# Another stored order for the same 1505 operations: 115 transfers and 451 engine operations move, 24 PSUM evictions change engine

## The chip, the cores and the metric

One core of one Trainium2 chip runs the whole kernel. The metric is the device time of one execution in microseconds (us). Times of before are three runs; one further execution was profiled.

## What is computed

Two independent layers on 2048 tokens of 640 channels, written side by side into one output of 2048 x 1280 (bfloat16).

- Layer A is a convolution layer. `k` goes through a causal filter of four taps per channel, is multiplied by `v`, then convolved along the sequence with a filter of full length (`ssm_k`, one per channel; the reference does it by FFT), a skip term `ssm_D` is added, and the result is multiplied by `q`.
- Layer B is segmented attention with a memory: 32 heads of 20 channels, four segments of 512 tokens. In each segment causal softmax attention within the segment is mixed, by a gate per head, with a read of a memory matrix that sums `phi(k) v` over the earlier segments (`phi(t)` is `t + 1` for positive t, else `exp(t)`).

```python
kv = k_shift * v                                   # A: short filter, then gate
y = irfft2(rfft2(kv_pad) * rfft2(ssm_k_pad))[:S] + kv * ssm_D
a = q * y
p = softmax(qs @ ks.T * scale + mask); a_dot = p @ vs     # B, one segment, one head
num, den = phi(qs) @ M, phi(qs) @ z + 1e-6
o = g * num / den + (1 - g) * a_dot
M += phi(ks).T @ vs; z += phi(ks).sum()
b = concat_heads(o) @ wo
```

## The kernel before

**Work.** Layer A is done in five blocks of 128 channels (`conv(dp)`, dp 0 to 4). A block loads `k` transposed into the tile `kr`, `v` into `vt`, the long filter into `kT`, runs the short filter as matmuls on TensorE (`ks`), transforms both signals with matmuls against the table `Wf` (`FX` for the signal, `FK` for the filter; eight PSUM results of 128x512 each, copied into the one buffer `F`), joins them with butterfly adds (`BX`, `BK`) and multiplies them (`P1` to `P3`, `YB`) on VectorE, and transforms back with `Wi` (`I`), times `q`. Layer B is done in eight units u (segment u // 2, head half u % 2). `project(u)` makes keys and queries (`P`, into `KQ`), values (`V`, into `Va`), transposes `KQ` by DMA into `KQT` (`KT`, one transfer for each of four token blocks t), makes the `phi` tiles and transposes them (`PT`), finds a bound for each key row, writes that bound into four strips of `KQT` by four small transfers (`rows`, one for each group of four heads), and updates the memory. `attend(u)` fills logits in PSUM by matmuls of 32 rows (`S`; three kinds: D for the diagonal, A and J for what lies below it), takes their exp on ScalarE into one of seven `ET` buffers, and multiplies with the values (`O`), then normalises on VectorE (`N`). `project_out(s)` transposes the segment's output (`oT`, by DMA; `ot` on TensorE in the last segment) and multiplies it with `wo` (`W`); `OB` stores it.

**Order.** The program does not call the engines while it walks these loops. A recorder notes all 1505 operations and what each one needs (`Recorder.add`, line 155). Then `Recorder.issue` (line 252) emits them in the order of a stored list (`ORDER`, line 996, compressed text). Every instruction of the page therefore stands at line 261. Each engine, and the one queue SP that issues nearly all transfers (201; four more go by POOL), runs its own instructions strictly in that order and waits at the head of its queue until what the instruction needs is there. A second list (`BASE`, line 1017) says which of the eight PSUM banks each of 471 groups of PSUM results uses: a group's first matmul waits until the group that had the bank before has been read. A third text (`EVICT`, line 993) has a digit for each of 227 copies from PSUM to SBUF (`evict`, line 405): 1 puts it on VectorE, 0 on ScalarE.

**Names.** An operation is named by its key and unit: `P/0/1` is the projection of unit 0, token block 1; `FK` and `FX` results are named by c from 0 to 3; `xt/0` to `xt/3` are the transposes of the first 512 rows of x on TensorE, whose copies make `xT`; `taps` is the four-tap filter transposed, from which ScalarE makes the filter matrices `skd`. Ten matmuls on zeros (`warm`) run at the start.

Of the kernel before, what the change touches and what calls it, by code (L numbers as in the profile page):

```python
# [995 lines left out]
ORDER = r"""
c-jrtgMttW5Czb=Gk0=rwrjI(+um&3wry{=YqM?Jwr#$5zT#w+Y?57aNKVNmxh0R}l_(NXTtrGs6^SI}q@v`L>Jn9=NgOF7p(MXlmGV+nk_aWQR+7{bAQdE|RFeV{Sqe%KEhI&?uv8XEKCPs6rKXsuRMxIiTWU#W
Ni5MNro@oa8cWJ(eyt%v(p?H@LP;gXw2qY3G*Vw`YC~x*^`x9;k=D{uifcCs(gxB<+DZ!vEw!|<l$177TboKh=^^bTtyIx;Qc-(J9c?9bwU0EBdfH6VOM5A$9i^(ql_FAH3Tl6;p*^Lr_LjcVLCWhO=_CWBn8cG|
l3cpT2<a@brG(Vi1d>RGNJA|u4K%C_mN7C=hRY~PDPd%s43)7mTB>OyEupJ*yo{6yQb>b!gErRcx<}S%d?~3-wTaHry|PjlX$tA4$t076lL|UfR%vscB$H)|?2`~(tW#yPY?AI;N@mDL-7l?lnrzbPazK`751p$s
rL`{AHabt6X<PlJEwsHJm6qB;=W9EiC0pg7bkd&MOBZNIJtlp1wj7qux=jwrHr=jAq__6bwc16y>Kxgj+hv^|my6O*Pe`!r)M2_=FUeI|p$m1m_SY>sK(EPMiDM&lr^K~gx>YaBX_+VEb-rAYcy>mX%Pxs(6Lp|2  # L1000
kli{#<J%57FN1WCuGif%Mx$A38>fq8uP&6NwnZ+;GTo<R^{gzG!MaSA>p3~5`!%Jdv7tIdPs&n>k5rb-qT6vjpp$f(PS;a1QV(i)nXEDFzKqsUn%Ex7bD5$`WQNYv>oQeu$qKn4H|4e**2j{>?#L{CDR<?NX0{`m
!B)#reIT<n0UpU~c_nM)jjWVJc2QqQR768Uq_DTLN)jQXWwQ11L@wz&$zoUZvOblha!sE}R@)$JB{9-lcDt&lb)CGIVV1)_N-`uzY&)w@bhw?-50V5S@>DlUPCKE`^ppl7DRS8-IjK`@gq_o=Hqr)KbX?FBh#<H1
yymvg5(9ZHrp2<<_#$bM#|GIqiHSS<Q19wjNrUV9NMqr#-q4$x4!884=CeMCjkkJVze|35pg&~1^|v^9r|<QZCbzU!!0yQ}iHiZ26|XhWe##roh<JFeza^bzLT3Dx43f>p+8>!<FSMY&)C86dAM}g<laKmU$5=uO
g-@CVpS7fY(}_0DfYO#8-!(J@KeUu(fFV03SxV$U8B2wqTGkZPtgscbB38+!8&S?8ps4jjWgBJ1tcp1zA}2;$aVuf7E!YNIE_A{Wt7>5|%Vt;}6h}3yZecOgCR+*Au-qt$APa|@79Qm-5{hAt<;7g9VEIrUg;5rz
QPE0bp1ri%))xVoZ-G+BDxe(dS`jR?0jOuStPB=eJ1d3yRuBQ~U_&iG8rV8pZ0)VJ^+!WnZ(t!Tu`rCxwicUhOxeOJVyO*8SjJ%#4na$+gk`qeMxd2d!3vAYMm7kQF%-iv5-V+i4Mt;YYE8`eTZf}6R#`QWG1=V4
U>us+Sj6H6tAUL+9^n`n9j%jvXJ-qs1YB)vY^`;%C@@RNuJ%{E8LczA+g9sg|Fox7M=$Gb+pLd?ZMXRB&P42Mn=A<va|$+FKXZ#j*cR)CP!@xCFqFG3G?TI)doTinFpSB$$EKn`yJG_O+78=i1+d?0;(-0piHOKR
*2Y1L#va&ZJFN@i@{mPmEhOU^i^qHDz&^Z-!`2gZ(3L58&d%B;>&trR#*`d|RJ>xBZ5q<B7mnHt)W<P9V#n=-rDjLY#7V1*(Ku!2tv9Bl0WMlZYY68gq-AKkV4>I*H!K~S;-=lQ!3?nG7{c2Y+3uKHW8AgLxM%Hn
)goDYUbFjXg!IhJ>z0uN*pv5dEHiOAnxGj@+hWYZ1AAnT?THQIQ=5%B2xFr-kip2pUR;9VoQs9%#0;E=wFqmYxdJ1&2wC~edb2Yh+Ip<R7`8)pF2xf(w`^R7hse!w+<<3zfc6;Ayd24ie2Ud*fjnG^HCTm7e2yG!
gPhF8`MANB$j1c;L4HnV7q-F_w#6k}Mr%x^djW>>f}GAG6feZ0gim8(7Go6Kh#7og#aW4=eI{REGfJ>BH=zpuvLv^lBevotI-mx__&5Gz5P$GHtFk74avQ4gJxg-}w__H|uq?~*Bdhb3T|q6DVtIbx96rJhd}19|
U@))ZG3K&1>vA?Dcmp<MBhF(*?!+}T<~O`S6E<aie!(vMVLgVk>-dhhXvRg{jfNi4!`oMUwi{^97Hr8@T+Hykg!8!vk-Rl;;<bITM*h*%7jgk3`&Yh#`7N~JC+x#gwq<*#f3nwjhbSK8x3Qe-xEB#@89R7XU(cGp  # L1010
9~&6L6?~7+*vMn}fK{yJoA?o{xsnI4mSH`bH}i0Q5NmiGwLQAOvwdvt@9hWnv%VkTQT)Ua1b7VJ%q`r?ZQRZV9@7uwAY=I<9O7ZN^&Q;FuNK=|czoZ@Jv@QE{DseK=dN-5H;(Wx{@@D(^dwsPQ6A$dgwns3*#F_p
{}GDkyLcM^40?)@HHp8qq#oDLK((uzez4O#i{tF#)Dt|zvka>z+0D-}wAS-5dY(NziiX#4n!qD!R6U2D9zoCJ7ZZ6Tji$-`0u%ZV>*W{O*?%*-CikBf=$CkzSD3<6`EN_<S9y(ptc~aQ>x`+ry^mi+L2v3Yw6Ul5
0^ZNRSsG90!t|cOGkR=|rD^@UHSs*2*ZX=t&*c5Rm1p(=UdV5<h+n`XX7y~I-Q#Kw&*FtWr^nG>*4m5uV?N+*=JMiR!i)Js-r^v?!%{xPOM4kF>*YM2j`Nb9+XwmtkFR%G-k-375BBl?ibMS#6KW;D&(}<#!@aUs
@$O#HhxrJv>Q7n66KN8y<|BQSKjUamtj}53$9Q$`=t;GcPxRC})?aXnPxVRulGA*;FZap*hRJk>ukac^(--<m-|ve(xz6@rpW}1=Ef4q-Po=Ybk*CzXo>7;28lC6!eV?!O6q-|)`38T-OuF7fe4{V$O&+MZbd_)R
b-u+9`XNuN>2$T{(af4&*Z5Z7=2>;S@9=E8(|7r9&!C5Wk00@io<(!(ZNKD4J-Z(B9D2s@_+7u}_x-G&^YebeFZ&h0>eu|b-|(A$%a8jBKk29ZwEqW|<?eI
"""
# [76 lines left out]
```

## Time and profile before

| what | value |
|---|---|
| three runs | 268.25, 268.42, 270.69 us; median 268.42 us |
| span of the profiled execution (first to last instruction) | 266.3 us |
| what lies around the span, if that execution took the median | 2.1 us |
| busy: TensorE matmul, VectorE, ScalarE, GpSimd | 257.8, 247.1, 248.8, 7.6 us |
| granted TensorE clock | 1.000 |

The page gives one time of its own, the span; the difference to a run's time lies before the first and after the last instruction. The busy times are unions: where one instruction starts before the last has left the engine, the overlap counts once. The chain is the list of work followed back from the last instruction, each step to what released it. A row of the timeline has the start, the time that the merged instructions took, the engine, the line, the operation, the tiles, and how many there are; an idle time before it and what ended it stand in brackets. The queue SP is SPq.

### The profile page before, as it was taken

Reading aid. Unit: us, or ns where it says so; the run is one execution under the profiler, and the core shown is the slowest. Engines: PE = TensorE matmul, PEld = TensorE weight load, DVE = VectorE, ACT = ScalarE, POOL = GpSimd, SP = SyncE. Lnnn points to the kernel's source line nnn. Section 1 sums busy time; section 2 is a strip of 40 time slices with the busy share of each in tenths; the row PEclk is TensorE's granted clock in tenths of the full one; section 3 lists DMA queues with packets and bytes.
Section 4 is the critical chain, followed back from the end, with each engine's and each line's share of the span. In section 5 each row is a group of like instructions: output and inputs, shape, how many; then the busy total and the mean of one; then the engine's idle time right before and its main releaser. Section 6 shows DMA issues by size and latency. Waiting matters only on the chain.

```text
span 266.3 us, 10034 instructions
## 1 busy us (share of the span) xinstructions
PE 257.8 (97%) x4323; PEld 193.0 (72%) x4323; DVE 247.1 (93%) x387; ACT 248.8 (93%) x392; POOL 7.6 (3%) x20
## 2 busy tenths in 40 slices
PE   7999999999999999999999999999999999988994
PEld 3788678778777778877767777778776876665871
DVE  0599999999999999999999999999999999999971
ACT  2878999999999999999999999999999999999953
POOL 8300000000000000000000000000000000000000
PEclk9999999999999999999999999999999999999999
...
GB/s 217 292 214 218 197 180 187 126 233 205 172 200 175 142 180 162 173 154 126 154 173 201 164 185 182 211 107 113 181 186 3 29 158 149 87 108 128 28 66 116
DMA packets 126604, 41.84 MB, mean 157 GB/s; under 512 B 114107, under 2 KB 125376, under 8 KB 126432
## 3 DMA queue, kind: packets, MB, share of 16 engines
...
## 4 chain that ended last, share of the span: by engine, by line
PE 62%; ACT 28%; DVE 5%; issue 2%; DMA 1%; POOL 0%; DVEq 0%; ACTq 0%; POOLq 0%
PE ps L261 62%; ACT ET L261 19%; ACT F L261 3%; ACT KQ L261 1%; ACT PP L261 1%; DMA qabs<-in_A_shift_k_dram 1%; ACT Va L261 1%; DVE vt L261 1%; ACT outb L261 1%; DVE Y L261 1%; DVE Kh L261 1%; ACT qabs L261 1%; DVE pq L261 0%; ACT xT L261 0%; DVE o L261 0%
## 5 line engine op out<-in xcount | busy, mean ns | idle before, releaser
L261 ACT ACTIVATE ET<-ps 128x1024 bf16<-128x1024 f32 x160 | 162.6, 1122 | 0.4 <-PE ps L261 0.2
L261 PEld LDWEIGHTS <-xT 128*128 128x128 bf16 x640 | 57.3, 98 | 27.8 <-issue 6.8
L261 PE MATMUL ps<-wqkv,xT 128*128 128x320 bf16 x480 | 77.0, 299 | 0.4
L261 ACT CAST F<-ps 128x512 bf16<-128x512 f32 x72 | 43.3, 686 | 0.9 <-DVE F L261 0.8
L261 PE MATMUL ps<-Va,ET 128*128 128x21 bf16 x1280 | 41.8, 173 | 0.0
L261 PEld LDWEIGHTS <-ET 128*128 128x128 bf16 x1280 | 39.1, 96 | 2.1 <-issue 1.0
L261 PE MATMUL ps<-KQT 32*128 32x128 bf16 (+3 forms) x896 | 35.7, 239 | 0.3
L261 PEld LDWEIGHTS <-Wf 128*128 128x128 bf16 x320 | 29.8, 98 | 6.1 <-issue 1.3
L261 ACT CAST KQ<-ps 128x320 bf16<-128x320 f32 x54 | 25.5, 513 | 2.4 <-PE ps L261 2.3
L261 PE MATMUL ps<-wo,xT 128*128 128x320 bf16 (+2 forms) x160 | 25.5, 299 | 1.3 <-ACT ET L261 1.3
L261 PEld LDWEIGHTS <-KQT 32*128 32x128 bf16 (+1 forms) x896 | 16.1, 92 | 9.9 <-issue 8.2
L261 PE MATMUL ps<-kT,Wf 128*128 128x256 bf16 x160 | 21.8, 273 | 0.1
L261 PE MATMUL ps<-vt,Wf 128*128 128x256 bf16 x160 | 21.2, 273 | 0.0
L261 PE MATMUL ps<-Y,Wi 128*128 128x256 bf16 x160 | 20.8, 273 | 0.0
L261 DVE TENSOR_TENSOR o<-ps,rr 128x640 bf16<-128x640 f32 x24 | 19.7, 819 | 0.4
L261 DVE TENSOR_TENSOR Y<-Y,pq 128x2048 bf16<-128x2048 bf16 (+1 forms) x20 | 18.6, 937 | 0.0
L261 PE MATMUL ps<-Mbd,PqT 128*128 128x84 bf16 x96 | 18.3, 203 | 0.1
L261 DVE TENSOR_TENSOR pq<-Xh,Kh 128x2048 bf16<-128x2048 bf16 x15 | 18.2, 1215 | 0.0
L261 PE MATMUL ps<-skd,kr 128*128 128x128 bf16 (+4 forms) x124 | 17.9, 270 | 0.0
L261 PEld LDWEIGHTS <-kr 128*128 128x128 bf16 x124 | 15.6, 147 | 2.5 <-issue 0.8
L261 PEld LDWEIGHTS <-Wi 128*128 128x128 bf16 x160 | 14.8, 98 | 2.5 <-issue 0.6
L261 ACT ACTIVATE PP<-KQ 128x1280 bf16<-128x1280 bf16 x12 | 15.9, 1361 | 0.0
...
## 6 DMA issues: line engine op xcount, KB each, us to landing
...
```

The lines of the kernel that those rows point to most:

```text
L261: f(*[fix(a) for a in args], **{k: fix(v) for k, v in kw.items()})
```

## The change

Nothing is computed otherwise and no instruction is added or removed, except that a copy on the other engine is another instruction there. Three stored texts are replaced:

```diff
-EVICT = ("10100001110000001000000010000000000000000000000000000000000000100000000000001000010001001010100110100000000000000000110000000000000010000000"
-         "000000000101000100100100000000000000010000001100001000000000000000000000010110010000100")
+EVICT = ("01001011001001000000010000000000000000000000000000000000000000100000000000001000010001001100110010100010000000000000010000000000000011000000"
+         "000000000101000100100100000000000000010000001000101000000000000000000000010110000000001")
 ORDER = r"""
-c-jrtgMttW5Czb=Gk0=rwrjI(+um&3wry{=YqM?Jwr#$5zT#w+Y?57aNKVNmxh0R}l_(NXTtrGs6^SI}q@v`L>Jn9=NgOF7p(MXlmGV+nk_aWQR+7{bAQdE|RFeV{Sqe%KEhI&?uv8XEKCPs6rKXsuRMxIiTWU#W
...
+c-jTQ17HvU6a>(_kF;zr+qP}DY}>YN+t#veEZes2_o5&xA|N6np)?$k0aQUYltV?NLTY434&+2G<VGIkMH*y8K2%43ltEM!Ks1y^RTM%s6hU4oh){@$@`!~>$b@{77?s3OSt_822#QK&lolc>YNIIXA`yzC4vLAQ
...
 BASE = r"""
...
```

Decoded and set beside the old lists:

- **EVICT.** 12 copies go from ScalarE to VectorE: xt/0, xt/3 (640 wide); kt/1, two of `FK`, one of `FX`, W/3/4 (512); P/0/0, P/0/1, P/1/0, P/2/3, W/2/2 (320). 12 go from VectorE to ScalarE: taps (40); xt/1 (640); kt/3, two of `FK`, one of `FX`, ot/3/2, W/3/2 (512); P/0/0 and P/0/2 (the other half of each), W/0/0, W/2/1 (320).
- **First 30 us.** On SP the first block of x goes from third place to first, so that the weights of `P` and then `ident` follow it; the four loads of `Wf` go 3, 1, 0, 2 in place of 3, 0, 2, 1. On TensorE xt/0 and the last of `warm` go ahead of `taps`, the gate's small matmul comes right behind `taps`, P/0/0 stays in its place with xt/1 and xt/2 behind it, and the second result of P/0/0 goes from ahead of `FK` to behind the short filter. ScalarE begins with the copy of `taps`, then the two exps of the gate, three `skd`, the copies of xt/1 and xt/2; before it began with one `skd`, xt/0, another `skd`, xt/3, the gate. On VectorE the four `ks` products come before the second of the `BK` steps.
- **Middle.** The order of the logits blocks `S` on TensorE is kept; between them the other matmuls are exchanged over a few places. 387 of 471 groups have another bank. On SP 95 of the 201 transfers are out of their old order, by up to 18 places: the transfer KT/3/0 goes from behind the copies and loads of block 3 (place 88) to between the first and the second `rows` of unit 2 (place 70), and of these four the one for head group 0, which was first, is now third, behind it; KT/4/0 goes behind four more copies of the filter of block 3 and the store OB/0/1; PT/3/3 goes from ahead of `rows` of unit 3 to behind them; oT/0/2 goes behind PT/4/3. On ScalarE one copy of P/5/0 into `KQ`, which needs KT/4/0 to have read that tile, goes five places ahead.
- **End.** The parts of the last `W` run in the order 2, 4, 3, 0, 1 (before 2, 4, 1, 3, 0), their stores likewise; I/2 goes ahead of ot/3/2 and I/0.

More of the change, by code (lines that the diff above doesn't have):

```diff
@@ L995 @@
 KQW, FW, WW = 1, 1, 1
 ORDER = r"""
-c-jrtgMttW5Czb=Gk0=rwrjI(+um&3wry{=YqM?Jwr#$5zT#w+Y?57aNKVNmxh0R}l_(NXTtrGs6^SI}q@v`L>Jn9=NgOF7p(MXlmGV+nk_aWQR+7{bAQdE|RFeV{Sqe%KEhI&?uv8XEKCPs6rKXsuRMxIiTWU#W
-Ni5MNro@oa8cWJ(eyt%v(p?H@LP;gXw2qY3G*Vw`YC~x*^`x9;k=D{uifcCs(gxB<+DZ!vEw!|<l$177TboKh=^^bTtyIx;Qc-(J9c?9bwU0EBdfH6VOM5A$9i^(ql_FAH3Tl6;p*^Lr_LjcVLCWhO=_CWBn8cG|
-l3cpT2<a@brG(Vi1d>RGNJA|u4K%C_mN7C=hRY~PDPd%s43)7mTB>OyEupJ*yo{6yQb>b!gErRcx<}S%d?~3-wTaHry|PjlX$tA4$t076lL|UfR%vscB$H)|?2`~(tW#yPY?AI;N@mDL-7l?lnrzbPazK`751p$s
@@ L1000 @@
[L1000 to L1012, printed above, removed]
@@ L1013 @@
-0^ZNRSsG90!t|cOGkR=|rD^@UHSs*2*ZX=t&*c5Rm1p(=UdV5<h+n`XX7y~I-Q#Kw&*FtWr^nG>*4m5uV?N+*=JMiR!i)Js-r^v?!%{xPOM4kF>*YM2j`Nb9+XwmtkFR%G-k-375BBl?ibMS#6KW;D&(}<#!@aUs
-@$O#HhxrJv>Q7n66KN8y<|BQSKjUamtj}53$9Q$`=t;GcPxRC})?aXnPxVRulGA*;FZap*hRJk>ukac^(--<m-|ve(xz6@rpW}1=Ef4q-Po=Ybk*CzXo>7;28lC6!eV?!O6q-|)`38T-OuF7fe4{V$O&+MZbd_)R
-b-u+9`XNuN>2$T{(af4&*Z5Z7=2>;S@9=E8(|7r9&!C5Wk00@io<(!(ZNKD4J-Z(B9D2s@_+7u}_x-G&^YebeFZ&h0>eu|b-|(A$%a8jBKk29ZwEqW|<?eI
+c-jTQ17HvU6a>(_kF;zr+qP}DY}>YN+t#veEZes2_o5&xA|N6np)?$k0aQUYltV?NLTY434&+2G<VGIkMH*y8K2%43ltEM!Ks1y^RTM%s6hU4oh){@$@`!~>$b@{77?s3OSt_822#QK&lolc>YNIIXA`yzC4vLAQ
@@ new lines @@
+27(X+Wu&a6Kyj&u%*cY8sD-v@iki|D<)kozq%~Ti85*KKYDsNrhsJ1yv}le-h>ki^5_P2wTA(}Ppa=S(0lJ|HN})Y^p)YzPCHkQ!5}-fwOBD%?PDqAgC?Fj$4(U);MqwCANj(WfTnxf+48dTGzyPGjP>exGbVe7H
+ka!q~@u(>EWh4qq4H=8_QcxO5H5rYP(oh;n7{o_dB*ZFdEE}beES3r~0TZ!FCSww&Vu=Jxby+QIWD2GsHuhqzG?i|$4>K@FHp^T&fF?2>-DN*o$x`Vdt)-b9L^w2;d9qB}$Y#vMd}%A~rG>PVW9T3|WEOtO0y&P^
+XeS-z5VoL`9Kk|aDV?RSY?DQD6x-!6dP*<pEq$bmtdq;=D(ht%F5(I<p`YxO4KfFFu}kLR1WsbN43jN#6~m>!Y?WPzqdPD{<|D2yzyKL2+ff2%FkY_VEOuidqUs)rr-NjIEXG9HE9VhSFW`WTk>#>aQfnGrgmDsI
+S4a{aE9bCZ_8_Tl#b6mCLnQ>uky4LKe5TS<*olL3NCL1FBju<Zkrh~iWk{qa<TOT0bR8x4F-a2ZLrjzFxPe=^iODiW4$B=(l^8l*j>$?qM+Qxf8IpjnF;i~i5oSq7eSq1LSy$l&GU-b^#w)DBT4d3S@&>DsLZ2WZ
@@ new lines @@
+1DS}I<Smlm9q!^Op5d}&zy<{B6<LR@nqIF-RBl9ey((wqJ<iE`MB^t6)8U$wPb9V`=0}{B9Qss(aZ-};ndH<DNWx7>&Qmf)b7=~mmJym;r)r1{)RFoH=jAglNK8%3L7JKmC6=b)V|gUkB^~o>Y~GeUdPnZc4Y?_|
+<eq#(T;|iScq{p}zrK@ryf5GJK>9E%?_q$xmsj#yGBP}V;3t0JH~!)e{(&5?$+VEZk+eENV=@!d>2t}<7m`4e>rnk7A7re4l$TOa6Y3}VELjK^(2|;sUuB$T(@>1T^!z5@<%g6~Wd=^v()v@fbCTwuF(qTMj0#gR
+G^2BxmenFUT`Orh4bRFNhefrDj?!Z4jKG{Mp?#T~Gjy;P)}qYCIU0t=b%@T?(HfR{I7W-HF#EBp&em!=S*vRet*Jqpk40Es2eN{`)NstphzwwP&ehslQA=~4&eupR!#Y}$3$!e2X<aSOdRmGVSc2`ezOL7DjAZ@U
+K^JKQZLb@2vF2w%Mz%s+qOEn7#<sRvkxO*|<5(M|g)y;Z8rE89D{ZO2C5o-k&RnilID{j(QY*2MMqyN2r9(NAl{t)^*jNW~IM?cGU8959M60o>Hq*##u4+{|j_Y&`$Fc^;Gp23Sa28;(ELb;bM@?vEowTziu!h=2
@@ new lines @@
+yQ=D6`6s5^bP9LqLfx+2G|=MPRQAxG+LIA2vGvjz)?2%4B7<&LY9HOI)wxAoLup?fYTd01_h>hEWfB`^J**~^SwHP(;ccJp)&90qCoqWnwFi^i9oFV<4Xp=smxi`poXA={sE0I~MYjl+)DCN0JF9){kKAJc9?^J~
+!a}rz-DOHUryZ>hyINnnq%$~;-K;lL*%htFx*Wx0n#NMwOkURGdQ_+Lgm&jiJ+G&9G~FWTMZKW)8BtGbLr!7?ik{K?Ol#?^F&puQ-qLn9*lz1&-qA>!(S}$PHseFy)tlOsp)9iA(@d7$?(0=;Z$0h0Uej58pd)Rp
+Wwzn=NFVDcd!kRZlMS$5Hk$)2gJrQfe5iA|j7#`TmvbpMa1lG(2wTk2_FS8DjLqi*hS7P<YAYC4v)MDQ;y7E!HOy}9_=KyulI!`LxosmCa=f+YT28b))`Cyj#d26)%VnF`hB+;tO|tyflC3z|+H#N;umx<*DR#r$
+LwP}i7qLP%)m~^(>unRPBa7KIn{I_Im@{mq(YLSzi(3h+WG`6R{#q5g%zw6-B`vgXV+{-AFS(U9?VJ6uC_3A|TU86P_g395v6OwZ9js=b>^8S^CreuyD{JMfmVK~!_S0tBBi6R^*1+al1*>C^xr=kGqBXQeR@WNa
@@ new lines @@
+7l!w6TF>fR6MMq|ZED~6O26_3cXO^q@LSx&#TL=ua;Y`+&$`6^*mr)>=5~`UEW9?eme$By*#cW+dnvxqTH8l$W3RZMpZJ=~tfpV#bw+me74}I3`~a6*6mRbx{HyKbdV9zBY->Tj!9LS`qiwQai|U(grLDGA_JLPf
+%h%Xi`^bX~>xcMGqj_`>=goYb)%K(Osz<orn)`d*YTIm!{opYkW=!91JFLDRw4HXqe)5nt@Wa;DWB4v>=PmpfWBCy~!98}8pDngW^4<1Y_t{>%#xHi9fBA<lrx?du`fnb!V|JQ<^$d?&D2eO;G?G9Pc|89|N)msg
+Z#A*2oMmJ&IbmJ=l*RY1e$vkIw4E`LHh$K+`8kUsp(Tujm2eVb=dH7U&;W@l;U$6h@Cz0}0==h4lo0;VgdR<P>Mu*`zwM%3vSi-NlY3J?&w3tRF54BmYS%1<r}E!=-Tr8P@9m8}ru6ZYet|Khp!fCE9$UU?0Z-@Y
+J(gT#T8G`V44%d_`giT;nLLm8_a@%TGy4F~=UF_i<n==S$O?NA&+6GcyXWwn-rav`9C>W5J(m~t;(pr(c`<)r@g%no^ub=jZ&_(C<7NG!mGe9H#7cQdALrvezTCC)o<Jt}E34qIZHN!`VSdjld1bHS38kV}^$|YY
@@ L1016 @@
+>-bX(lu<s?t9f<5Z;9oZC6duz*E{-iOCm39jF0t+-pP~7OPlOde5z0L=|0I<_$r^_Z)~O4@R@$VlgUA!<%@i_r;#~6*XQ|LTkK1GsW11Gvd>dVYT54@Wxg-)WxmcAdQREsDP+BG@=Ox!n?09o@YSANvdR|U>Urdl
+uk|&aP2O2r+3wpsogDTZzSDR45kKk|J%^;1+n!nO_-?=Cdwj1S^DJ`BkNb7M;khM)-1U2&U2ggbzw9Udir?~6e%9~%X+P&z{fvkBdB5QQ0cjxabN
 """
 BASE = r"""
-c-mc30kQ=l2qH7P|Bb%^HT(YTw3QJeIRFd<sz+jRy?dN_c64=g_q;oTp3i@FZ1$>p9(|HVZ-8vexIrYy61*|F0uj5v$#^nzP{qkt%qZ3%W{_Dok{Dq(H71#r0akn%z}00Jclvx$gQ@^)TGSeh?zfxH6-23;AWyw`
-GIDlB{xWvhS!ov&h=r?#|M|G__KO;hF6kM(S=4$QIhkND<bo948P26xGGo5nVNc4hxwzjS4d5wUc|FGXSBGkq=gZwN=<DsC!5i{ii1N6e#&bEJpTGK5VbBdR*N<D$R8}UvVRi9&tDtL19a6U4NyYE>db(@z-nc&e
@@ L1020 @@
-zj<yB_0_Fy+ZU-_pF7vVd_53;{d!F5fS_B_eBS8~RvQK@
+c-lph3lhX22tyGN?|<W!N9>Mcs|ZQ>n7QTM%fiZzZO-Rzzu&m`<Xf_~@77DP=RUD<Z+1`pEfAe$L^no(d$@J{#y^O3-o`7hz27>rSs#aA&x3t94m<~)c2CJ_mb&*u!$do=j&GqL$$Enn=t+DG?yiG<mS$O;oYz!V
+CDu_LRAZt8UBlC!8{fyZKGaZEQn(NGh-vaR^<p%QEs5H!pqc?<f^4e%DEfCK;WYOC7$$cIajEi+xIlg0gFjl9ctf)?D5lvsnk$!OP!DsEnxpvo<f?Z_b*l1-j>&$>bK+gK8lKcdyb3$omU{Wm^i5~6p3<#~Ze_92
+S6{COIX`9p|M2FgIE8UwdEZiH3cTq~YJwiin_1WFyYhNHSXAK$+zSRt
 """
```

## The prediction

> **What bounds the kernel now.** I read the page first, then the busy time by stretches, then the chain in order of time, then the timeline of the first 30 us, of the queue SP, and of the end.
>
> ```profile
> span 266.3 us, 10034 instructions
> ...
> PE 257.8 (97%) x4323; PEld 193.0 (72%) x4323; DVE 247.1 (93%) x387; ACT 248.8 (93%) x392; POOL 7.6 (3%) x20
> ...
> PE 62%; ACT 28%; DVE 5%; issue 2%; DMA 1%; POOL 0%; DVEq 0%; ACTq 0%; POOLq 0%
> ```
>
> ```profile
> 100.00:120.00 20.00, 20.00 (x316) 16.09 (x319) 19.92 (x34) 20.00 (x33) 0.00 (x0) 1.00 0.90 163
> ...
> 140.00:160.00 20.00, 20.00 (x349) 15.52 (x348) 19.96 (x32) 20.00 (x35) 0.00 (x0) 1.00 0.97 183
> ```
>
> The second fence has stretches of 20 us: busy TensorE, weight loads, VectorE, ScalarE, GpSimd, then the granted clock, the share of the DMA engines and GB/s. Three engines are busy for at least 19.9 of 20 us and the DMA engines for nine tenths. No single engine bounds this kernel: each nearly fills the time, and the chain steps between TensorE (62%) and ScalarE (28%). An order can gain only what the three lose together, at the start and at the end. In the middle it has little to win, and one late hand-over can hold all three.
>
> **The change part by part.** No operation is added, so the cost lies in waits, and in copies that take another time on the other engine. I go from the start to the end.
>
> *The first 10 us.*
>
> ```profile
> 1.24 0.51 SPq L261 DMA_DIRECT2D ident<-c_ident  x1
> 1.79 1.85 SPq L261 DMA_DIRECT2D Y<-in_B_x_dram  x4
> ...
> 4.51 1.28 ACT L261 ACT_TABLE_LOAD   x1 [4.51 <-DMA ident<-c_ident]
> ...
> 5.52 0.62 PE L261 MATMUL ps<-ident,qabs 5*64 5x5 bf16 x12 [0.67 <-DMA qabs<-in_A_shift_k_dram]
> ...
> 6.08 0.45 PE L261 MATMUL ps<-ident,Y 128*128 128x128 bf16 x5
> 6.18 0.20 DVE L261 COPY taps<-ps 128x40 f32<-128x40 f32 x1 [4.98 <-PE ps L261]
> ...
> 6.42 0.40 ACT L261 ACTIVATE skd<-ident,taps 128x128 bf16<-128x128 bf16 x1 [0.63 <-DVE taps L261]
> ...
> 6.72 0.67 ACT L261 CAST xT<-ps 128x640 bf16<-128x640 f32 x1
> ...
> 7.34 0.82 DVE L261 CAST xT<-ps 128x640 bf16<-128x640 f32 x1 [0.96 <-PE ps L261]
> 7.45 0.52 PEld L261 LDWEIGHTS <-xT 128*128 128x128 bf16 x5 [0.32 <-ACT xT L261]
> ...
> 8.63 1.53 PE L261 MATMUL ps<-wqkv,xT 128*128 128x320 bf16 x10
> ```
>
> ```profile
> 7.45 44.03 PE ps L261 x556
> ```
>
> The last row is of the chain: from 7.45 to 51.48 the end hangs on TensorE without a break. So the start is worth what it does to TensorE. Before, the first block's transpose waited behind `taps`, whose input landed at 5.5; its copy by ScalarE ended at 7.39 and the projections began at 7.45. Now the transpose goes first. It needs `ident`, which landed by 4.5 and is now issued behind the block of x, 0.5 us later; with that block's bytes ahead of it I put it at 5.6, an estimate from these issues. Transpose until 6.1, VectorE's copy of 0.82, so P/0/0 at 7.0: 0.45 us earlier. Against it stands ScalarE. The table load stood directly before the first ACTIVATE and behind that one's wait for `ident`, hidden in the wait for `taps`. Now ScalarE's first operation is a plain copy of `taps` (0.20, from about 6.6) and the first ACTIVATE is the gate's exp behind it, so the load's 1.28 us begins at 6.8 and hides nothing. Then two exps (about 0.1 each), three `skd` (about 0.3 each, by the 0.40 less overlap) and the copy of xt/1 (0.67): ready at 9.7. P/0/1 needs it and started at 8.63. TensorE has P/0/0, two transposes and P/0/3 to do first (ten matmuls took 1.53, so 0.7 a group, and 0.3 a transpose): 7.0 + 0.7 + 0.6 + 0.7 = 9.0. It then waits until 9.7 and ends P/0/1 at 10.4. Before, the same work ended at 10.0, when the filter's transposes began. **TensorE is 0.4 us late.** Bounds: 0.3 early, if the load comes early after all (xt/1 ready at 8.4, no wait); 1.3 late, if the whole load passes on.
>
> The Trainium skill bears on this row ("ScalarE: Activation LUTs", section "What ACT_TABLE_LOAD costs"): the load takes about 1283 ns and a drain of some 1380 ns goes with it. The row's 1283 ns agree; no drain shows here, since ScalarE then waited for `taps` anyway. By the page the load would cost 2.66 us at its new place, and TensorE would be 1.8 us late and not 0.4.
>
> *10 to 30 us.*
>
> ```profile
> 18.17 1.22 DVE L261 TENSOR_TENSOR Kh<-F 128x2048 bf16<-128x2048 bf16 x1
> ...
> 22.51 1.22 DVE L261 TENSOR_TENSOR F<-F 128x2048 bf16<-128x2048 bf16 x1
> ...
> 27.77 1.23 DVE L261 TENSOR_TENSOR Xh<-F 128x2048 bf16<-128x2048 bf16 x1
> ```
>
> ```profile
> 19.94 0.42 ACT L261 CAST KQ<-ps 128x320 bf16<-128x320 f32 x1 [1.81 <-PE ps L261]
> ...
> 23.84 1.56 ACT L261 CAST F<-ps 128x512 bf16<-128x512 f32 x3 [0.80 <-DVE F L261]
> ```
>
> ScalarE loses 1.81 and 0.80 us here, the second because the buffer F is free only when VectorE's step of 22.51 has ended. In the new order the four `ks` products come ahead of one step of 0.7 us, so that step and the copies behind it come some 0.5 us earlier, and so may the one of 27.77. TensorE runs through all of this, so for the end I count nothing; a full gain is a rival below.
>
> *Transfers that come later.* Between the stretches above, the order on SP changes most. A transfer that lands late holds whatever waits for it, and all that is queued behind that on its engine.
>
> ```profile
> 28.54 1.31 SPq L261 DMA_DIRECT2D KQT<-qabs  x2
> ...
> 84.35 0.62 SPq L261 DMA_DIRECT2D KQT<-qabs  x1
> ...
> 89.71 1.24 SPq L261 DMA_TRANSPOSE KQT<-KQ  x1
> ```
>
> ```profile
> 106.35 2.91 SPq L261 DMA_TRANSPOSE KQT<-KQ  x1
> ...
> 111.24 4.03 SPq L261 DMA_TRANSPOSE PqT<-PP  x1
> ...
> 132.98 1.31 SPq L261 DMA_TRANSPOSE KQT<-KQ  x1
> 134.34 0.71 SPq L261 DMA_DIRECT2D kT<-kT  x1
> 135.09 1.40 SPq L261 DMA_TRANSPOSE xT<-o_s  x1
> ```
>
> ```profile
> 31.86 0.23 PEld L261 LDWEIGHTS <-pack 32*128 32x128 bf16 x16 [0.26 <-issue]
> ```
>
> ```profile
> 85.34 0.48 ACT L261 CAST KQ<-ps 128x320 bf16<-128x320 f32 x1
> ```
>
> ```profile
> 91.66 0.52 PE L261 MATMUL ps<-pack 32*128 32x128 bf16 x15
> ```
>
> ```profile
> 139.87 0.84 ACT L261 CAST KQ<-ps 128x320 bf16<-128x320 f32 x2
> ```
>
> ```profile
> 143.92 0.85 PE L261 MATMUL ps<-wo,xT 128*128 128x320 bf16 x5
> ```
>
> How long a landing takes: the first two `rows` of unit 0 were issued in the 1.31 from 28.54, so the first by about 29.2, and the logits that need it began at 31.86: 2.6 us at most.
>
> Place one is KT/3/0, in the row of 106.35. It now stands ahead of the `rows` transfer for group 0 (row of 84.35). It must wait for ScalarE's copy that ends at 85.8, then takes 1.24 to 2.91; two `rows` of 0.6 follow; so issued by 88.2 to 89.9 and landed by 90.8 to 92.5. TensorE's S/2/0/D wants it at 91.66: 0 to 0.9 us late, and behind it stand all matmuls.
>
> Place two is around 130. PT/3/3 (4.03) has moved behind the `rows` of unit 3, four more filter copies of 0.7 stand ahead of KT/4/0, and a store of 0.5. One load of 2.3 went ahead in exchange, so KT/4/0, issued by 134.3 before, comes 3.6 to 4.8 later: 137.9 to 139.1. With a landing of 2.6 to 3 it has read `KQ` at 140.5 to 142.1. ScalarE's copy of P/5/0 is moved to about 139.9 and cannot begin before: 0.6 to 2.2 us of ScalarE, with exps and copies queued behind it, for which TensorE's banks wait. oT/0/2 (135.09) comes behind PT/4/3 and lands at 144.3 to 147.4; W/0/3 wants it at 144.6, at its new place 0.7 behind the row of 143.92: 0 to 2.8 late. The two overlap, so place two costs 0 to 2.8, not the sum.
>
> Together 0 to 3.7 us. I take 0.6, near the lower end: these transfers had 5 us and more in hand before, my bounds add up the longest issues, and a hold of a few tenths on one engine is given back where another was the later one.
>
> *Copies on the other engine.* A 640-wide copy takes 0.82 on VectorE against 0.67 on ScalarE. Behind the first 30 us VectorE gains three copies of 320 and loses two until the end, 0.4 us in all, and ScalarE loses as much. VectorE has 5% of the chain: I take 0, bounds -0.4 (ScalarE on the chain) and +0.4.
>
> *The end.*
>
> ```profile
> 258.65 4.06 PE L261 MATMUL ps<-wo,xT 128*128 128x512 bf16 x24
> ...
> 262.75 0.58 ACT L261 CAST PP<-ps 128x512 bf16<-128x512 f32 x1 [0.49 <-PE ps L261]
> ```
>
> TensorE runs the last 24 matmuls without a gap, then one copy and one store. The new order does the same matmuls and a copy of 0.6 is last again: 0.1 less, as one matmul is taken forward into a wait; bounds 0.6 to either side, a copy's length.
>
> **Sum.** +0.4 + 0.6 + 0 - 0.1 = +0.9 us on the span of 266.3, so 267.2. The median of the runs, 268.42, is 2.1 above the span, and the same lies around it after: 268.42 + 0.9 = **269.3 us**. Taking every bound, the likeliest case itself runs from 268.42 - 0.3 - 0.4 - 0.6 = 267.1 to 268.42 + 1.3 + 0.6 + 0.4 + 0.6 = 271.3.
>
> **The rivals.**
>
> *The late transfers pass on in full.* Places one and two hold TensorE and ScalarE for 3.7 us: 268.42 + 0.4 + 3.7 - 0.1 = **272.4**. For it: the engines are full, so nothing takes a hold up. Against it: before, hardly any wait for a transfer shows behind the start. It decides from 2.4 us of hold on, which puts the time over 271.1. Place two alone can do that.
>
> *The table load passes on in full* and the transfers as I took them: +1.3 + 0.6 - 0.1, so **270.2**. For it: nothing now stands before the load that ScalarE could be waiting for. Against it: TensorE has other work for most of it.
>
> *Faster.* The order is a better fit: ScalarE's gaps of 1.81 and 0.80 close, the engines follow, the load costs nothing (-0.3): 268.42 - 2.6 - 0.3 = **265.5**. For it: ScalarE and VectorE do come earlier between 15 and 28. Against it: TensorE has no gap there to give, and three full engines would have to gain at once.
>
> **How the numbers follow.** Forecast 0.46, table load 0.15, late transfers 0.28, faster 0.11. A measurement of this kernel tells about 1% from no change, 2.7 us: faster is below 265.7, slower above 271.1. Only the last rival is faster: 0.11. The transfers' rival is slower, less a hundredth for its near end: 0.27. The rest, 0.62, is within 1%. The range for 8 in 10 leaves out the far half of each outer case: 266.2 to 272.4.
>
> **What would show it.** The table load at 6 to 8 us, behind the copy of `taps`; P/0/0 before 7.2 and P/0/1 after 9.3; the step of 27.77 some half a us earlier. In the list of waits, a wait of S/2/0 or W/0/3 on TensorE for a transfer, or ScalarE idle ahead of a copy into `KQ` near 140, shows places one and two; none there takes 0.6 out of the sum. A table load that ends before 6, or a middle (30 to 245) that is shorter or longer by over 2 us without these waits, makes the prediction wrong.

## The result, and the profile after

Seven runs of the changed kernel have a median of 270.96 us (270.13 to 272.50). Seven runs of the kernel before beside them have 268.51 us. The ratio is 1.0088, with a 95% interval of 1.0059 to 1.0117: the change costs 2.45 us, slightly less than the 1% that was called no change, and it goes the way of the forecast (+0.9 us). The profiled execution took 271.77 us, 0.8 us more than the median, so its lines add up to more than 2.45 us. The profile of before lies on the other side: executions of that kernel with its span of 266.3 us took 268.1 us, 0.4 less than the median. So 1.2 of the 3.7 us that the two spans differ by are those two executions. One of the profiles used below, that of the kernel `mended`, is of a disturbed execution (273.66 us where the median is 269.33), and only its last 10 us are read.

The page of the changed kernel: the span, the busy times, and the chain by engine.

```profile
span 270.0 us, 10052 instructions
...
PE 256.5 (95%) x4323; PEld 192.7 (71%) x4323; DVE 248.9 (92%) x387; ACT 249.4 (92%) x392; POOL 7.5 (3%) x20
...
PE 53%; ACT 29%; DMA 7%; issue 4%; DVE 3%; SPq 2%; ACTq 0%; DVEq 0%
```

The span is 3.7 us longer at about the same busy times: the loss is waiting. The chain has 7% of transfers where it had 1%. Next, busy time in two stretches of the changed kernel, and after it in the same stretches of the kernel before. The columns are TensorE, weight loads, VectorE, ScalarE, GpSimd, the granted clock, the share of the DMA engines, GB/s.

```profile
0.00:10.00 10.00, 8.74 (x62) 4.89 (x63) 3.52 (x7) 4.45 (x14) 7.53 (x20) 1.00 0.82 242
...
20.00:40.00 20.00, 18.93 (x224) 14.18 (x226) 18.91 (x26) 15.65 (x33) 0.00 (x0) 1.00 0.91 181
```

```profile
0.00:10.00 10.00, 7.93 (x58) 4.53 (x59) 1.75 (x4) 4.29 (x9) 7.59 (x20) 1.00 0.81 240
...
20.00:40.00 20.00, 20.00 (x233) 15.05 (x232) 19.79 (x29) 18.57 (x43) 0.00 (x0) 1.00 0.95 198
```

TensorE does more in the first 10 us (8.74 against 7.93) and loses 1.07 between 20 and 40.

**The first 10 us are better than before.** The timeline of the changed kernel:

```profile
0.73 1.28 ACT L261 ACT_TABLE_LOAD   x1 [0.73 <-PEq L1077]
...
6.52 0.19 ACT L261 COPY taps<-ps 128x40 f32<-128x40 f32 x1 [4.50 <-PE ps L261]
...
6.85 0.85 PE L261 MATMUL ps<-wqkv,xT 128*128 128x320 bf16 x5
```

```profile
8.10 2.20 PE L261 MATMUL ps<-wqkv,xT 128*128 128x320 bf16 x15
...
12.47 2.46 PE L261 MATMUL ps<-kT,Wf 128*128 128x256 bf16 x21
```

The table load runs at 0.73, as the first thing that ScalarE does. The forecast put it behind the copy of `taps`, at 6.8. Before, it carried the wait of the first ACTIVATE (for `ident`, 4.51); now ScalarE's first operation is a plain copy, the load stands ahead of that one and has no wait but the start of the program. So xt/1 is ready in time, the fifteen projection matmuls from 8.10 run without a wait, and the filter matmuls `FK` begin at 12.47. Before, they began here:

```profile
13.69 0.27 PE L261 MATMUL ps<-kT,Wf 128*128 128x256 bf16 x1
```

Of the 1.22 us of difference, one projection that now comes later accounts for 0.7; the gain is 0.5.

**From 16 to 34 us this turns into a loss.** TensorE, ScalarE and the queue SP of the changed kernel, one fence each:

```profile
17.06 3.77 PE L261 MATMUL ps<-skd,kr 128*128 128x512 bf16 x28 [0.83 <-DMA kr<-in_A_k_dram]
...
33.83 0.40 PE L261 MATMUL ps<-KQT 32*128 32x128 bf16 x16 [1.07 <-DMA KQT<-qabs]
```

```profile
21.54 0.42 ACT L261 CAST KQ<-ps 128x320 bf16<-128x320 f32 x1 [3.26 <-PE ps L261]
```

```profile
16.49 8.13 SPq L261 DMA_TRANSPOSE KQT<-KQ  x4
...
25.95 3.95 SPq L261 DMA_TRANSPOSE kr<-in_A_k_dram  x1
30.13 0.69 SPq L261 DMA_DIRECT2D KQT<-qabs  x1
```

The same queue before:

```profile
16.68 6.33 SPq L261 DMA_TRANSPOSE KQT<-KQ  x4
...
24.35 3.95 SPq L261 DMA_TRANSPOSE kr<-in_A_k_dram  x1
```

Read it backwards from the wait at 33.83. The logits of S/0/1/D, the first block, wait 1.07 us there for the `rows` transfer that was issued at 30.13; before, the first `rows` began at 28.54. SP issues in order, and the load of `kr` ahead of it stood at 25.95 in place of 24.35. That is late because the four KT transposes ahead of it end at 24.6 in place of 23.0. They are late because ScalarE's copy into `KQ` is made at 21.54, after 3.26 us in which ScalarE waited for TensorE. And TensorE was late with that result because the four short-filter results `ks` now stand ahead of the last two projections of unit 0 (28 matmuls, 3.77 us; before, two of them stood ahead of the last result of P/0/3 and none ahead of that of P/0/0). TensorE reached the `ks` so early that `kr` had not landed: 0.83 us of wait. An order change on TensorE has gone by ScalarE to SP, and 17 us later TensorE waits for a transfer of SP. That the later issue makes this wait is not shown yet: the transfer was also long under way, 3.70 us from its issue to the logits, and the runs below show it issued as late without a wait.

**The late transfers, in the middle.** The timeline of the changed kernel at places one and two, and at a third one:

```profile
93.59 0.43 PE L261 MATMUL ps<-pack 32*128 32x128 bf16 x15
```

```profile
137.36 1.38 SPq L261 DMA_TRANSPOSE KQT<-KQ  x1
...
142.10 1.16 ACT L261 CAST KQ<-ps 128x320 bf16<-128x320 f32 x3
```

```profile
190.07 0.42 ACT L261 CAST KQ<-ps 128x320 bf16<-128x320 f32 x1 [0.54 <-DMA KQT<-KQ]
```

```profile
185.00 4.96 DMA KQT<-KQ
```

At place one, S/2/0/D starts at 93.59 without a wait, 1.93 late, no later than the blocks around it. At place two, KT/4/0 is issued by 138.7 (forecast: 137.9 to 139.1), yet ScalarE comes to the copy of P/5/0 at 142.10 only, without idle time. The third place was not named: the copy of P/7/1 waits 0.54 us for KT/6/1. The last fence is of the chain: that transfer was issued at 185.00 and landed 4.96 us later. It has the same place among SP's transfers as before (the 148th), but others stand ahead of it.

Small waits are in the list of waits, in which the columns are total, times and the longest; first after, then before:

```profile
PE ps L261 <- ACT ET L261: 4.2, 12, 0.5
```

```profile
PE ps L261 <- ACT ET L261: 1.9, 5, 0.5
```

**The end.** ScalarE's last copy and SP's stores after, and SP's before:

```profile
265.75 0.58 ACT L261 CAST PP<-ps 128x512 bf16<-128x512 f32 x1 [0.44 <-PE ps L261]
```

```profile
258.34 6.28 SPq L261 DMA_DIRECT2D out_dram<-pq  x7
264.72 0.55 SPq L261 DMA_DIRECT2D out_dram<-PP  x1
265.37 0.39 SPq L261 DMA_DIRECT2D out_dram<-outb  x1
265.86 1.49 SPq L261 DMA_DIRECT2D out_dram<-PP  x3
```

```profile
260.60 0.77 SPq L261 DMA_DIRECT2D out_dram<-outb  x1
261.47 2.22 SPq L261 DMA_DIRECT2D out_dram<-PP  x4
```

The last copy ends at 266.33 after, 3.0 later than before (263.33). From there to the end of the span it is 3.67 us where it was 2.97: twelve stores now follow each other on SP without a break, and SP is still issuing earlier ones when the last copy is done. Before, SP was idle between them. The first of the twelve are stores of A/4/O/2 and A/4/O/0, which go ahead of those of A/4/O/1 now; the list of the change does not name this.

**Where it went, in this profile.** Lag is how much later TensorE starts the same block of logits than in the profile of before, from the rows of both timelines:

```
                     S/0/0/A   S/3/1/A   S/3/3/A   S/5/1/A   S/7/3/A   span
before, starts at      34.09    134.57    150.07    193.11    253.11   266.3
after, lag              1.74      1.80      2.21      2.79      3.02    +3.7
```

So 1.7 us of 3.7 is lost before 34 us, 0.4 near 140 to 150, 0.6 around 190, 0.2 behind that, and 0.7 at the end.

### The profile page after: what moved, and what is told of

It is laid out like the page before. It is cut to its first block, busy times and chain, and to the rows that moved or that the text cites. A ratio compares the mean times of both kernels' runs of the same rounds, so it can differ in the third digit from the quotient of the medians.

```text
span 270.0 us, 10052 instructions
## 1 busy us (share of the span) xinstructions
PE 256.5 (95%) x4323; PEld 192.7 (71%) x4323; DVE 248.9 (92%) x387; ACT 249.4 (92%) x392; POOL 7.5 (3%) x20
## 4 chain that ended last, share of the span: by engine, by line
PE 53%; ACT 29%; DMA 7%; issue 4%; DVE 3%; SPq 2%; ACTq 0%; DVEq 0%
PE ps L261 53%; ACT ET L261 20%; DMA kr<-in_A_k_dram 4%; ACT F L261 3%; SPq L261 2%; ACT Va L261 2%; DMA KQT<-KQ 2%; ACT KQ L261 2%; DMA KQT<-qabs 1%; ACT PP L261 1%; ACT outb L261 1%; DVE Xh L261 1%; DVE pq L261 1%; DVE F L261 0%; DVE PP L261 0%
## 5 line engine op out<-in xcount | busy, mean ns | idle before, releaser
L261 ACT ACTIVATE ET<-ps 128x1024 bf16<-128x1024 f32 x160 | 160.7, 1108 | 1.3 <-PE ps L261 1.2
L261 PE MATMUL ps<-wqkv,xT 128*128 128x320 bf16 x480 | 76.2, 299 | 0.8 <-ACT ET L261 0.3
L261 PE MATMUL ps<-KQT 32*128 32x128 bf16 (+3 forms) x896 | 33.1, 239 | 2.1 <-DMA KQT<-qabs 1.1
L261 ACT CAST KQ<-ps 128x320 bf16<-128x320 f32 x52 | 24.4, 509 | 4.6 <-PE ps L261 4.0
L261 PEld LDWEIGHTS <-KQT 32*128 32x128 bf16 (+1 forms) x896 | 15.4, 92 | 10.5 <-issue 9.2
```

What stands on the lines that cost most here:

```text
L261: f(*[fix(a) for a in args], **{k: fix(v) for k, v in kw.items()})
```

## The experiments

The theory after this reading: (1) the `ks` in front cost the start, by KQ, KT and `rows`; (2) late transposes in the middle hold ScalarE; (3) the stores at the end back up on SP. The main rival: the orders lose by many small waits, without a place. In all runs, a ratio is to the kernel before, measured beside it on the same chip. Two ratios of different sets have an uncertainty of some 0.004 against each other (0.0030 and 0.0029 added as squares), 1.1 us.

### Only one part of the order: the start or the rest

```diff
 old_start: each engine and SP
+order of before, up to S/0/0/D (37 us)
 order of after, from there
 new_start: the other way round
```

> The order of before up to the logits block S/0/0/D (the first 37 us), with its copies and banks, and the order of after from there on. Theory 1 (most of the loss arises in the first 36 us: in the trace of after TensorE is 1.74 us behind at S/0/0/A): that loss is gone, what is left is what the later part adds, some 0.7 us by the medians (2.45 - 1.74), so about 269.2 us. Rival (the start is only moved waiting, the full engines of the middle would have made the same up, and the loss belongs to the later transfers): 270.4 to 271.0, as after.

> The reverse: the order of after up to S/0/0/D, that of before from there on. Theory 1: the 1.7 us of the start stay, so 268.5 + 1.7 = 270.2 us, and TensorE is some 1.7 us later than in before from S/0/0/A to the end. Rival: 268.5 to 269.0, as before.

`old_start`: median 271.03, ratio 1.0071 (1.0046 to 1.0096). `new_start`: 269.79, 1.0041 (1.0016 to 1.0067). Neither part holds the loss alone. But the cut makes a wait of its own, as here in `old_start`, where S/0/0/D on TensorE waits 1.03 us for an exp:

```profile
37.03 0.39 PE L261 MATMUL ps<-pack 32*128 32x128 bf16 x16 [1.03 <-ACT ET L261]
```

Its lag is 0.04 at S/0/0/A and 0.97 at the next but one, S/0/0/J. `new_start` has a lag of 0.94 at S/0/0/A, a wait of 0.7 at the cut, and then 1.56 to 1.60 at every block from 41 us to the last. With the old order behind it, the start's loss is neither given back nor added to.

Both were built a second time, to move the cut. As built they moved little: `old_start_2` has the order of `old_start` on every engine and on SP, and `new_start_2` the engines' order of `new_start`.

```diff
 old_start_2: old_start
-second half of S/0/0/D in PSUM banks 3 and 4
+second half of S/0/0/D in PSUM banks 0 and 1
 new_start_2: new_start, on SP
+rows/0 (head group 2)
 load of wqkv, rows/0 (head group 3), A/1/sk (both)
-rows/0 (head group 2)
```

> As old_start, with the cut one block later (behind S/0/0/D), because the first cut made a wait of its own: 1.03 us of TensorE at S/0/0/D for a bank that ScalarE still read. Theory 1 (the start is the larger part): TensorE runs level with before up to 130 us (lag 0 to 0.3), ends 0.7 to 1.3 late, and the time is 268.5 + 1.0 = 269.5 us. Rival (the later part costs as much with or without the late start): the lag grows to 2 us or more by 250 us, 270.5 us.

> As new_start, with the cut behind S/0/0/D. Theory 1: a constant lag of TensorE between 0.9 (the first new_start had 0.94 at S/0/0/A and made 0.8 more at its cut) and 1.7 us (after), from 36 us to the end; 269.4 to 270.2 us. Rival (full engines of the middle take a late start up): the lag falls below 0.5 by 130 us, 268.5 to 269.0.

`old_start_2`: 270.80, 1.0108 (1.0070 to 1.0147); `new_start_2`: 270.14, 1.0053 (1.0027 to 1.0080). So the cut was not moved, and these are near repeats; the ratios of the first two differ by 0.0037. The waits at the cut are there again: 1.03 us in `old_start_2`, for the exp of S/0/0/A, which holds the bank of the first half of S/0/0/D, and here in `new_start_2`:

```profile
38.45 0.36 PE L261 MATMUL ps<-pack 32*128 32x128 bf16 x13 [0.70 <-ACT ET L261]
```

So the time of a half order can be read only less its cut. The two with the new start stand 1.1 and 1.4 us above before (0.0041 and 0.0053 of 268.5); less 0.70 each, **the start costs 0.4 to 0.7 us**. By the lag at S/0/0/A it costs 0.94 and 1.60 in their profiles; 0.4 of that is the profile of before, which is so much faster than its median.

### The four `ks` behind the projections

```diff
 TensorE: ... FK
+P/0/0 (second result), P/0/3 (last result), in other PSUM banks
 ks/0, ks/2, ks/1, ks/3
-P/0/0 (second result), P/0/3 (last result)
 FX ...
```

> The kernel after with one thing changed: the last group of P/0/0 and of P/0/3 go ahead of the four ks products of block 0 on TensorE, as P/0/0 and P/0/3 did before. Theory 1a (ks comes so early that TensorE waits 0.83 us for kr, and the two projections behind it are late for ScalarE's copies, for KT/0/0 and KT/0/3, for A/1/lk on SP and for the rows transfers): the wait for kr is filled, SP's A/1/lk begins near 24.4 in place of 25.95, the wait of S/0/0/A for a rows transfer (1.07) shrinks or goes, and the time falls by 0.8 to 1.7 us: 269.3 to 270.2. Theory 1b (the loss at S/0/0/A is the order of the rows transfers on SP alone): at most the 0.2 of the start is given back, 270.7 to 271.0.

Median 270.23, ratio 1.0069 (1.0039 to 1.0099). The times do not tell it from after; the timeline does. TensorE and SP in `ks_behind`:

```profile
21.91 0.27 PE L261 MATMUL ps<-vt,Wf 128*128 128x256 bf16 x1 [0.49 <-DVE vt L261]
22.52 1.36 PE L261 MATMUL ps<-vt,Wf 128*128 128x256 bf16 x11 [0.33 <-DVE vt L261]
...
32.98 0.39 PE L261 MATMUL ps<-KQT 32*128 32x128 bf16 x16
```

```profile
16.23 6.26 SPq L261 DMA_TRANSPOSE KQT<-KQ  x4
...
23.82 3.85 SPq L261 DMA_TRANSPOSE kr<-in_A_k_dram  x1
29.99 0.69 SPq L261 DMA_DIRECT2D KQT<-qabs  x1
```

The four transposes take 6.26 us again and the load of `kr` is at 23.82. The waits for `kr` and for `rows` are gone. So the chain from `ks` by KQ to the load of `kr` on SP is shown. It does not go on to the issue of `rows`: that is at 29.99, nearly as in after (30.13), because SP sat idle from 27.67 until ScalarE's copy of the bounds was done, and yet the logits at 32.98 did not wait for it. And only half the lag goes (0.87 at S/0/0/A in place of 1.74): the `ks` products on VectorE are later now, and TensorE waits 0.82 us for `vt`. A wait in another place has come in.

How firm the chain is shows in all profiles of the study together, without that of `mended`. KT x4 is the time of the four transposes on SP, then come the issue of the first `rows` and TensorE's wait for it.

```
                 start of          KQ copy    KT x4   rows at   its wait   lag at S/0/0/A
before           before            19.94      6.33    28.54     0          0
old_start        before            19.98      6.51    28.46     0          0.04
old_start_2      before            19.93      6.31    28.44     0         -0.01
old_start_kt     before            19.88      6.35    28.84     0         -0.06
old_start_3      before            21.31      8.09    29.80     0          1.38
best_start       see below         17.95      6.41    28.24     0         -0.21
after            after             21.54      8.13    30.13     1.07       1.74
new_start        after             20.92      7.67    29.46     0.90       0.94
new_start_2      after             21.62      8.13    29.98     0.85       1.60
kt_early         after             21.10      7.91    29.89     1.47       1.70
rows_back        after, see below  20.89      7.76    29.61     1.32       1.33
sp_back          after             21.64      8.13    30.16     0          0.58
ks_behind        after, ks behind  18.20      6.26    29.99     0          0.87
```

With the new start the copy is never earlier than 20.89, whether TensorE waited for `kr` or not. With the old one it is at 19.9, but for one execution, in which `ks` began at 18.66 and not at 17.3: the old order can lose the same 1.4 us, only not as a rule. The last step is the weak one. Five of the six executions with the new start and the late copy wait for `rows`, and the sixth, `sp_back`, which up to there has after's orders, does not, though SP issued the transfer as late as in after:

```profile
30.16 0.68 SPq L261 DMA_DIRECT2D KQT<-qabs  x1
```

```profile
32.69 0.39 PE L261 MATMUL ps<-KQT 32*128 32x128 bf16 x16
```

Here it was there 2.53 us after its issue at the latest, in after only 3.70 us after it. So what makes the wait is how long the transfer was under way, not when it was issued. That the late load of `kr` just ahead of it makes this longer fits with `ks_behind` and not with `sp_back`; the cause stays open.

### The `rows` transfer ahead of the load of `vt`

```diff
 SP: ... A/1/lk, rows/0
+rows/0 (second)
 A/1/lv
-rows/0 (second)
```

> The kernel after with one transfer moved: the rows transfer of group 0 (unit 0) goes back ahead of the load A/1/lv, directly behind the first rows transfer, as before. Theory 1b (the order on SP makes S/0/0/A wait): it issues 0.65 us earlier, the wait of 1.07 falls to 0.4, and the time falls by about 0.6: 270.3. Theory 1a (SP reached the rows 1.6 us late because of the projections behind ks): the same 0.6 us at S/0/0/A at most, and what follows stays late, so 270.3 to 271.0; the two are told apart by ks_behind being the larger.

Median 270.55, ratio 1.0082 (1.0051 to 1.0113): no change against after. The waits in `rows_back`, and SP:

```profile
PE ps L261 <- DMA KQT<-qabs: 1.3, 1, 1.3
ACT KQ L261 <- DMA KQT<-KQ: 0.9, 1, 0.9
```

```profile
29.61 1.31 SPq L261 DMA_DIRECT2D KQT<-qabs  x2
```

The `rows` wait stays, 1.3 us long, though both transfers are now issued without the load between them. That theory falls: the order behind A/1/lk is not the cause. The second row is new: place two as forecast. KT/4/0 was 0.7 us later in this execution, and ScalarE's copy of P/5/0 waits for it:

```profile
138.14 1.28 SPq L261 DMA_TRANSPOSE KQT<-KQ  x1
...
142.66 1.08 ACT L261 CAST KQ<-ps 128x320 bf16<-128x320 f32 x3 [0.85 <-DMA KQT<-KQ]
```

From the end of the issue (139.42) to the copy it is 3.24 us. By the same 3.24 us, KT/4/0 of after, issued by 138.74, would have read `KQ` at 141.98, 0.12 us before ScalarE comes to the copy at 142.10: place two was hidden there by about a tenth of a microsecond, an estimate from these two rows.

### SP in its old order

```diff
 all engines: order of after
 SP, from the 34th transfer on
-order of after
+order of before
```

> The kernel after, with every transfer on SP from place 33 on (from 40 us) in the order of before, and all four engines as in after. Theory 2a (the prediction's: what the part behind 40 us loses, it loses by transfers that land late, such as KT/6/3, for which ScalarE waited 0.54 us at 190): the lag from 137 us on stays at its value of 130 us, 1.0 to 1.3 us less at the end, 269.7 us. Theory 2b (it loses by the order on the engines: copies ahead of the exps on ScalarE, for which TensorE waits 4.2 us in place of 1.9): only the 0.54 goes, 270.4 to 271.0; or slower, if the engines now want a transfer sooner than the old order brings it.

Median 280.49, ratio 1.0455 (1.0430 to 1.0481). The waits:

```profile
PE ps L261 <- DVE KQ L261: 4.4, 1, 4.4
...
ACT KQ L261 <- DMA KQT<-KQ: 3.7, 2, 2.3
```

Each is larger than any wait of these two engines in after behind the first 30 us, and the lag is 9.0 us at S/1/1/A (65 us). The order of the transfers belongs to the order of the engines; exchanged as a block it says nothing about single places of the change. As a test it was too coarse.

### The two late transposes forward

```diff
 SP:
+KT/4/0
 A/4/lk, OB/0/1
-KT/4/0
 ...
+rows/5 (last), KT/6/1
 A/4/ss/4
-rows/5 (last)
 A/4/ss/6
-KT/6/1
```

> The kernel after with two transposes taken forward on SP: KT/4/0 ahead of the load A/4/lk (about 2.5 us sooner), and KT/6/1 with one rows transfer ahead of the filter copies A/4/ss/4 and ss/6 (1.4 us sooner). Theory 2a (late transposes hold ScalarE's copies into KQ: 0.54 us idle ahead of the copy of P/7/1 at 190 in after; 0.50 to 1.03 ahead of the copy of P/5/0 near 142 in ks_behind, old_start_2 and rows_back): both waits are gone, ScalarE's idle time between 37 and 250 us falls below 0.3, and the time falls by 0.5 to 0.8 us, to about 270.3. Theory 2b (these holds are given back by the full engines): waits gone or not, the time stays at 270.8 to 271.0.

Median 270.38, ratio 1.0058 (1.0027 to 1.0088). In `kt_early` SP issues KT/6/1 at 183.48 and ScalarE copies P/7/1 without idle time:

```profile
183.48 1.67 SPq L261 DMA_TRANSPOSE KQT<-KQ  x1
...
189.36 0.57 ACT L261 CAST KQ<-ps 128x320 bf16<-128x320 f32 x1
```

The lag at S/5/0/J (189.73 before) is 2.25 in place of 2.70, and stays 0.4 smaller to the end (2.62 against 3.02). The same edit was made on a kernel with the old start, cut at 43 us.

```diff
 old_start_3:  order of before up to 43 us, then order of after
 old_start_kt: old_start_3
+KT/4/0 and KT/6/1 forward, as in kt_early
```

> Before's order up to 43 us on TensorE, after's from there; the cut lies where no bank is handed over in haste, since both earlier cuts at 36 us had made a wait of 1.03 us of their own. If start and later part add up (start 1.0 to 1.7, later part 1.3 by the traces): TensorE level with before at 44 us, 1.0 to 1.4 us late at 250, 269.4 to 269.9 us. If the later part costs the same whatever the start (it is bound by itself): 270.5 to 271.

> Both: before's order up to 43 us, and the two transposes taken forward in the rest. What is left is then only the small waits: ScalarE's instructions between 37 and 250 us start a few hundredths later each, 0.6 us in all by the traces (extra time of 7.15 us in after against 5.82, less the 0.8 of the transpose). If so: 268.5 + 0.6 = 269.1 us, TensorE 0.4 to 0.8 late at 250. If the order on the engines costs nothing (as predicted): 268.4 to 268.7.

`old_start_3`: 271.00, 1.0072 (1.0044 to 1.0099); `old_start_kt`: 269.82, 1.0032 (1.0014 to 1.0050). Measured side by side, the edit is worth 1.2 us by the medians, 0.0040 by the ratios (uncertain by 0.0033), and 0.6 us by the lowest times of each. In the two traces the lag grows by 0.93 and by 0.61 us from S/1/1/A to S/7/3/A. So **the late transposes cost 0.3 to 0.5 us in a trace, 0.8 and 1.1 by the times**; the 0.8, which is `kt_early` against after, is within its uncertainty of 0.004. That the times say more fits with place two, which shows in some executions (`rows_back`) and not in others: `old_start_3` waits 0.2 us for it, `old_start` 0.6 us at the copy of P/7/1 like after, and no profile shows both.

The cut at 43 us makes a wait as well, 0.60 and 0.59 us of TensorE for an exp at 45.68 and 44.25. The 0.86 us that `old_start_kt` has over before (0.0032, uncertain by 0.0018) are this wait and 0.3 us for all else, with the small waits and the end in it.

### The best start

```diff
 order of before, but
+the first 10 us of after
+P/0/3 (last result) ahead of all four ks
```

> The order of before, with the first 10 us as in after (first block of x first, taps copied by ScalarE so that the table load stands at 0.7 us, xt/0 ahead of taps) and the last group of P/0/3 ahead of the four ks products. Theory 1a (after's first 10 us are a gain, TensorE reaches the filter's matmuls some 0.5 us sooner with the same work done; it was lost behind them, at kr): TensorE 0.3 to 0.6 us earlier from 20 us to the end, 267.9 to 268.2 us. Rival (the start is bound by the landing of kr near 17 us and by the rows transfers near 31): TensorE 0 to 0.2 us earlier from 31 us on, 268.3 to 268.6.

Median 268.13 against 268.44, ratio 0.9989 (0.9972 to 1.0005). The lag is -0.21 at S/0/0/A and -0.22 at S/7/3/A. The new first 10 us, with P/0/3 ahead of the `ks`, are a small gain, and the gain lasts; it is too small to be told from no change. No version of the study is shown to be faster than the kernel before.

### All repairs together

```diff
 after
+ks_behind
+kt_early
 SP, at the end:
+A/4/O/1 (both), A/4/O/3 (second)
 A/4/O/2 (first), A/4/O/0 (first)
-A/4/O/1 (both), A/4/O/3 (second)
```

> The kernel after with three mends at once: the last groups of P/0/0 and P/0/3 ahead of the four ks products (as ks_behind), the two transposes forward on SP (as kt_early), and three stores of the last block's result (A/4/O/1 twice, A/4/O/3), ready by 255.9 us, ahead of the store A/4/O/2 that waits until 258.3, so that SP does not issue twelve stores without a break at the end, where in after the last store is issued 0.61 us behind its copy and 0.03 in before. If the terms add up: 270.96 - 0.5 (ks_behind) - 0.8 (transposes) - 0.5 (stores) = 269.2 us; from the end of the last copy to the end of the span 3.0 to 3.2 us in place of 3.66. If the stores' delay is the queue's and not their order: the end stays at 3.4 to 3.7, and 269.7 us. If the first two share one cause: 270.0 or more.

Median 269.33, ratio 1.0033 (1.0013 to 1.0054): 1.5 us of the 2.45 are back (0.0055 of the ratio, uncertain by 0.0036). In its last 10 us SP is idle again ahead of the last five stores:

```profile
260.11 4.58 SPq L261 DMA_DIRECT2D out_dram<-pq  x7
266.38 0.34 SPq L261 DMA_DIRECT2D out_dram<-PP  x1
```

```profile
268.31 0.58 ACT L261 CAST PP<-ps 128x512 bf16<-128x512 f32 x1 [0.44 <-PE ps L261]
```

From the end of the last copy (268.89) to the end of the span (271.9) it is 3.0 us, as before. That the order of the stores does this is not shown by it: in the other profiles with after's order of the stores this stretch takes 3.0 us (`rows_back`), 3.1 (`old_start_3`), 3.2, 3.3, 3.4, 3.4 and 3.6, and after's 3.67 is the longest. So the end costs 0 to 0.7 us, by the execution. The 0.9 us that are left are not settled: the rest of the start (0.87 in the trace of `ks_behind`) could fill them, and so could the waits for exps. No run separates the two.

## Why the prediction was right or wrong, by its steps

- **What bounds the kernel** (right). Three full engines, so an order loses by a late hand-over and gains only at the ends. `new_start_2` shows it best: 2.23 us of lag from the cut on, and 2.23 at the last block.
- **The first 10 us, +0.4 for the table load** (wrong). P/0/0 came as forecast (6.85 against 7.0). The load came at 0.73 and cost nothing, so P/0/1 did not wait. The text had said that a load that ends before 6 makes the prediction wrong, and here it does. The step took the load to stand ahead of the first ACTIVATE that needs the table; the run shows it ahead of ScalarE's first operation, with that one's wait. On the Trainium skill ("ScalarE: Activation LUTs", section "What ACT_TABLE_LOAD costs"): its 1283 ns agree with the row's 1.28 us; the drain that it names could not be seen, as ScalarE had 4.50 us of waiting behind the load. The 1.8 us by that page did not come.
- **10 to 30 us, nothing** (wrong in its reason). The step counted VectorE's and ScalarE's gains from the earlier `ks` and then said that TensorE runs through. It did not ask what the four `ks` on TensorE push back: the last results of P/0/0 and P/0/3, and with them KT and the load of `kr`. Its VectorE step came 0.2 us earlier (27.59), not 0.5. **This is the step that failed**: what is queued behind an instruction that moves forward. That the start costs about as much as forecast (0.4 to 0.7 by the times) is chance: the term was +0.4 for another cause.
- **Late transfers, +0.6** (mechanism right, size about right). Place one cost nothing. Place two waits in some executions, in after's profile not. A third transfer, KT/6/1, is of the same kind and was not named. Together 0.3 to 1.1 us, inside 0 to 3.7. The step set SP's new times against a ScalarE that is on time (139.9); it came to that copy at 142.10, as the whole kernel was some 2 us late by then, and that lateness was the cover.
- **Copies on the other engine, 0** (right). Behind the first 10 us VectorE is busy for 245.4 us in both profiles (247.1 - 1.75 and 248.9 - 3.52), ScalarE for 244.5 and 245.0. What the exchange of places adds is waits, not work: TensorE's waits for exps went from 1.9 to 4.2 us. The forecast had no term for these; that they cost a few tenths of a microsecond is argued from the lag between 34 and 150 us and from the 0.3 us of `old_start_kt`, and not shown by a run of its own.
- **The end, -0.1** (wrong, by a little more than its bound). The matmuls end as forecast, with a copy of 0.58 last, but the step counted the matmuls and copies and not the stores queued on SP: +0.7 in after's profile, 0 to 0.6 in the seven others with these stores in this order. That this order does it is argued, not shown.
- **The sum.** +0.9 was forecast, +2.45 was measured. The range, 266.2 to 272.4, held it. The three terms, 0.4 to 0.7, 0.8 to 1.1 and 0 to 0.7, make 1.2 to 2.5; their uncertainties are as large as they are.
